# Loading every block of q and k in 2 KB runs and keeping the tokens in (j r) order

## The chip, the core and the metric

The kernel runs on one core of a Trainium2 chip. The core has five engines with their own instruction queues: TensorE (PE in the profile; its weight loads are listed apart as PEld), VectorE (DVE), ScalarE (ACT), GpSimd (POOL) and SyncE (SP), which here only issues DMAs. Engines meet through semaphores alone. The metric is the device time of one execution in microseconds (us), lower is better.

## The reference, cut to what matters

Two layers follow each other. The first is causal attention that keeps, for each query, only the best six chunks of 32 keys; the second is a gated feed-forward layer over the 3072 resulting rows. All inputs and the output are fp32.

```python
# q, k, v: (4, 8, 768, 64): batch, heads, tokens, head_dim
k_min, k_max = min and max of k over each chunk of 32 tokens      # 24 chunks
ub = sum_d maximum(q * k_min, q * k_max)                          # a bound for each query and chunk
ub = where(query's chunk >= chunk, ub, -1e9)
top_chunks = argsort(ub)[..., -6:]
scores = q @ k.T / 8, masked to the selected chunks and to earlier tokens
attn_out = softmax(scores) @ v

x = attn_out as (4 * 768, 512)
xn = x / sqrt(mean(x * x) + 1e-6) * rms_g
out = (silu(xn @ w_gate) * (xn @ w_val)) @ w_out                  # 512 -> 1536 -> 512
```

## The kernel before, in words

The work is cut into 12 blocks: a batch `b` and 256 of its 768 tokens (`m` is 0, 1 or 2), in the order of the list ORDER (L341); `i` is a block's place in that list. For each block and each of two groups `g` of four heads the kernel does the following.

- **Load** (load_qk, L427). A block of q or k is brought to a tile of 128 partitions: four heads of 32 partitions, and for each the two groups, eight values `j`, and 64 numbers. For the first three blocks (PACKED, L351) partition `r` of a head takes the eight consecutive tokens 8r to 8r+7, a run of 2 KB in memory: four DMAs of 128 KB bring one tensor. For the nine other blocks partition `r` takes the tokens 32j + r, eight runs of 256 bytes: eight DMAs of 64 KB. All but those of block 0 are issued by SP. `load_v` brings v.
- **Turn** (L635). DVE transposes 32 by 32 squares, so that the 64 numbers lie on partitions and the tokens along the columns. Column 32j + r then holds token 32j + r in the nine blocks, which is token order, and token 8r + j in the packed ones, which is called (j r) order.
- **Copy to bf16** (half, L640 to L645). ACT or POOL writes `kb` and `qb` in token order; in the packed blocks its read runs over the columns with a step of 32 floats.
- **Choice of chunks.** DVE takes the minimum and maximum of k over each chunk (L650). TensorE multiplies them in fp32 with q and with the positive part of q (relu, L729) (upper_first, L539, for m = 0, upper, L521, for the others), DVE picks the six best and makes a mask from them.
- **Scores** (unit, L763). `kb` is the stationary operand, 128 keys, `qb` the moving one, 128 or 256 queries; four heads run side by side, on 32 partitions each. The mask is added in the same accumulation (L774). ACT takes the exponential (L813), POOL cuts the triangle (L783), TensorE multiplies with v (L839), DVE normalizes.
- **Feed-forward.** The row norm, a transpose of the rows (by TensorE in the first four blocks, by DMA, L899, in the others), the two wide products (L963), tanh on ACT, the products on DVE and POOL (L974 to L984), the output product (L1008) and a store by SP (L1030).

The order is not made by loops at run time. A planner has written down one list of all steps (SEQUENCE, L21), the buffer that each step takes (SLOTS), which engine does a step that several could do (CHOICE), and where matmuls without use stand that keep TensorE busy while it would wait (WARM, keep_busy, L1073 to L1076: place in the list, number, PSUM buffer, 1 for 512 columns and 0 for 128). Plan.run (L201) replays the list. Each engine executes its steps in that order and waits where an operand or a buffer is not ready. The numbers in the calls (0.54, 1.0 and so on) are the planner's costs in us for a step; at run time they have no effect.

Of the kernel before, what the change touches and what calls it, by code (L numbers as in the profile page):

```python
# [12 lines left out]
AXX = mybir.AxisListType.X  # L13
# [8 lines left out]
    29, 3, 4, 5, 44, 45, 0, 14, 21, 32, 6, 7, 34, 37, 35, 36, 64, 15, 17, 31, 55, 57, 65, 12, 16, 23, 13, 26,  # L22
    24, 19, 22, 8, 66, 67, 58, 68, 56, 59, 69, 46, 38, 39, 40, 41, 1, 28, 131, 27, 25, 30, 60, 61, 2, 70, 47,
    62, 71, 63, 72, 105, 106, 107, 147, 73, 96, 138, 140, 150, 148, 52, 53, 48, 49, 50, 51, 42, 43, 97, 139,
    129, 74, 82, 54, 83, 130, 18, 33, 132, 133, 20, 98, 145, 149, 75, 141, 156, 76, 142, 146, 84, 165, 166,
    167, 151, 99, 152, 85, 143, 144, 108, 77, 100, 101, 78, 102, 79, 103, 80, 109, 157, 154, 158, 159, 160,
    161, 162, 111, 110, 81, 104, 86, 87, 88, 112, 90, 113, 116, 135, 89, 93, 91, 92, 117, 94, 95, 118, 168,
    164, 173, 114, 174, 115, 175, 153, 213, 215, 214, 216, 155, 188, 189, 179, 187, 180, 181, 163, 124, 119,
    190, 217, 218, 220, 219, 125, 126, 120, 134, 191, 223, 182, 232, 183, 184, 225, 185, 234, 127, 121, 122,
    123, 128, 169, 196, 1078, 170, 171, 1080, 1084, 197, 198, 235, 186, 1086, 1079, 1082, 226, 172, 202, 192,  # L30
    194, 193, 1081, 230, 1083, 1087, 1072, 1074, 176, 1073, 1085, 227, 137, 228, 203, 204, 1076, 239, 177,
    1075, 236, 237, 261, 178, 195, 241, 229, 238, 242, 1088, 243, 262, 263, 205, 199, 1090, 224, 1089, 200,
    201, 206, 207, 208, 1092, 264, 1093, 265, 209, 1091, 1117, 1096, 1120, 1094, 210, 1102, 136, 231, 1077,
    1095, 1098, 1099, 240, 1104, 211, 1105, 244, 245, 266, 1097, 1100, 296, 301, 302, 288, 290, 298, 293, 289,
    299, 292, 291, 294, 295, 450, 303, 300, 297, 457, 372, 374, 379, 377, 376, 458, 375, 221, 1101, 1103,
    1116, 1106, 1107, 233, 1118, 1119, 1134, 1122, 1136, 1124, 1137, 1125, 246, 247, 315, 306, 308, 317, 1135,
    1129, 1128, 1138, 248, 1130, 1121, 1146, 250, 1148, 1132, 1149, 309, 267, 310, 268, 313, 1123, 251, 1126,
    253, 364, 378, 373, 222, 369, 304, 1147, 1140, 1150, 270, 316, 1142, 271, 273, 324, 1151, 318, 322, 254,
    1127, 311, 319, 1143, 325, 249, 1141, 1108, 1109, 1144, 320, 321, 10, 307, 272, 252, 269, 1145, 387, 312,
    274, 397, 1131, 1110, 1133, 1139, 1112, 255, 256, 275, 276, 257, 277, 1113, 1114, 278, 258, 368, 367, 365,  # L40
    371, 454, 366, 370, 451, 380, 456, 305, 463, 1115, 460, 259, 279, 260, 280, 281, 282, 389, 323, 283, 9,
    326, 327, 328, 1152, 1153, 382, 285, 329, 384, 330, 390, 392, 331, 393, 385, 394, 332, 395, 314, 284, 286,
    383, 287, 1111, 464, 544, 453, 461, 455, 452, 381, 1156, 1157, 1166, 1158, 1168, 1154, 399, 386, 396,
    1169, 334, 335, 337, 1184, 1172, 346, 1186, 1185, 1160, 1174, 347, 345, 349, 1162, 402, 462, 1155, 549,
    403, 545, 459, 400, 465, 401, 536, 539, 548, 333, 391, 336, 398, 338, 348, 350, 1188, 1187, 468, 1189,
    1175, 1161, 342, 1164, 470, 1163, 343, 344, 1165, 1167, 1170, 354, 339, 1190, 355, 476, 340, 356, 341,
    473, 1171, 1178, 1192, 1180, 388, 1193, 1181, 483, 1173, 1176, 1179, 351, 352, 353, 1182, 413, 404, 405,
    406, 1183, 471, 407, 408, 409, 410, 411, 1191, 469, 466, 1159, 542, 467, 538, 537, 475, 1177, 1196, 358,
    357, 359, 361, 360, 485, 1194, 362, 1195, 428, 363, 1200, 1197, 412, 429, 430, 432, 540, 546, 635, 541,
    543, 554, 556, 481, 479, 1204, 1201, 1222, 1202, 1198, 1206, 472, 478, 480, 547, 639, 488, 550, 551, 487,  # L50
    486, 212, 638, 489, 559, 568, 1203, 433, 482, 1207, 414, 1224, 415, 1216, 1205, 1208, 1223, 1226, 417,
    1218, 477, 474, 490, 434, 431, 491, 561, 11, 555, 570, 514, 627, 632, 634, 642, 574, 552, 637, 641, 629,
    573, 562, 1209, 1225, 564, 1219, 1227, 565, 492, 493, 494, 495, 496, 435, 436, 563, 630, 572, 633, 628,
    571, 1199, 416, 569, 418, 566, 484, 1217, 1210, 1220, 499, 419, 1212, 1213, 420, 421, 440, 1211, 1229,
    497, 557, 1214, 1232, 425, 437, 422, 426, 441, 427, 438, 442, 1215, 558, 1228, 423, 424, 439, 498, 444,
    1230, 1234, 567, 1231, 443, 1236, 576, 575, 636, 640, 1237, 650, 660, 505, 1235, 1238, 577, 506, 507, 500,
    445, 1221, 1233, 631, 1239, 578, 446, 579, 645, 1240, 501, 503, 515, 713, 718, 643, 715, 720, 653, 447,
    719, 553, 502, 504, 652, 560, 516, 518, 508, 511, 1241, 448, 647, 1242, 648, 509, 519, 662, 520, 521, 522,
    517, 449, 644, 664, 656, 510, 1244, 526, 1245, 1266, 1246, 580, 512, 581, 513, 527, 528, 582, 584, 1268,
    1255, 523, 1269, 530, 583, 1254, 649, 524, 525, 655, 1256, 529, 665, 666, 657, 812, 654, 646, 651, 531,  # L60
    1272, 1257, 658, 1274, 1275, 659, 593, 1267, 1261, 532, 534, 1258, 594, 595, 1273, 1264, 1276, 1278, 1270,
    721, 724, 726, 722, 717, 723, 663, 667, 668, 728, 727, 819, 1280, 725, 816, 716, 714, 1271, 1281, 533,
    535, 585, 691, 586, 588, 1260, 1279, 669, 590, 1282, 591, 592, 1277, 676, 587, 739, 736, 745, 738, 747,
    740, 1259, 1283, 670, 731, 733, 742, 1292, 1294, 1295, 734, 1305, 589, 1248, 603, 1262, 1308, 604, 606,
    596, 1298, 1300, 1250, 1263, 741, 597, 598, 671, 605, 749, 751, 750, 748, 752, 743, 599, 1293, 1296, 1301,
    1297, 602, 735, 1265, 607, 804, 1243, 810, 813, 814, 906, 1304, 1306, 808, 806, 898, 805, 811, 600, 732,
    746, 661, 744, 1251, 1307, 1309, 608, 609, 610, 1317, 1310, 1299, 1320, 1302, 1312, 672, 601, 807, 809,
    822, 673, 997, 904, 817, 998, 890, 900, 892, 818, 896, 1247, 895, 815, 905, 902, 899, 901, 893, 891, 611,
    612, 613, 674, 1249, 1252, 1253, 1313, 1311, 1314, 1315, 824, 830, 1316, 675, 617, 677, 678, 614, 831,
    679, 753, 1047, 823, 1318, 615, 616, 680, 620, 1284, 618, 619, 835, 833, 1319, 621, 825, 827, 754, 682,  # L70
    755, 837, 622, 1303, 683, 737, 829, 839, 1288, 1285, 684, 1286, 1322, 1324, 894, 989, 897, 991, 903, 623,
    908, 832, 1289, 1323, 697, 913, 826, 1325, 625, 840, 993, 624, 843, 907, 841, 698, 699, 1321, 681, 688,
    689, 756, 757, 910, 690, 909, 834, 626, 1332, 1290, 1326, 692, 693, 695, 915, 1029, 1291, 1287, 842, 1327,
    1328, 758, 759, 760, 836, 1329, 1333, 685, 762, 696, 922, 924, 694, 1330, 1334, 763, 729, 703, 916, 686,
    704, 705, 687, 700, 701, 702, 1336, 1361, 1360, 845, 764, 828, 838, 844, 765, 1338, 1339, 706, 707, 1364,
    1362, 1363, 767, 846, 768, 769, 1366, 1343, 1368, 981, 987, 730, 779, 990, 911, 847, 848, 708, 766, 761,
    780, 781, 783, 1346, 914, 1337, 1342, 1344, 1340, 770, 709, 711, 849, 1369, 1341, 1345, 850, 992, 1331,
    927, 996, 994, 928, 926, 925, 988, 985, 983, 710, 995, 1004, 1335, 930, 1365, 771, 1349, 1352, 772, 1354,
    1348, 1350, 1351, 1367, 1370, 1371, 1006, 917, 1356, 1355, 776, 777, 1357, 1013, 773, 774, 778, 1358, 782,
    1347, 785, 820, 982, 821, 786, 787, 986, 712, 984, 1380, 775, 1359, 1392, 1381, 1384, 784, 1394, 1382,  # L80
    851, 918, 1383, 1395, 919, 852, 788, 789, 1411, 1387, 1390, 1414, 790, 1410, 1353, 912, 1385, 920, 921,
    1015, 853, 929, 923, 1412, 1376, 794, 1413, 1415, 1005, 868, 795, 796, 859, 1377, 1378, 1404, 791, 792,
    793, 798, 860, 861, 797, 1406, 931, 869, 870, 1398, 872, 1400, 932, 933, 799, 1407, 1399, 1393, 854, 1402,
    1014, 1396, 800, 934, 802, 1397, 1401, 935, 855, 857, 936, 1386, 1372, 1405, 1408, 1019, 801, 803, 856,
    956, 999, 1016, 1018, 1017, 937, 858, 944, 1388, 1389, 1409, 865, 862, 866, 867, 863, 864, 945, 946, 1443,
# [1023 lines left out]
```

## Time and profile before

| | us |
|---|---|
| three runs | 305.08, 305.93 (median), 309.50 |
| profiled execution, its device time | 305.02 |
| its span, first to last instruction | 303.3 |
| TensorE busy | 287.6 |
| VectorE busy | 222.4 |
| ScalarE busy | 207.4 |
| GpSimd busy | 150.8 |

The granted TensorE clock was 0.994 of full speed. The core read 28.58 MB from memory and wrote 6.29 MB. The page cuts the span in 40 slices, and shows the DMA engines 70 to 90% and more busy in the first six and under 60% in nearly all that follow. In the profile an instruction is named by its line in the kernel, its engine, its operation and its tiles, output first; "idle before" is the time its engine stood still just ahead of it, and the name behind the arrow is what ended that. The chain is the path of work and waits that ended last, followed back from the last instruction.

### The profile page before, as it was taken

To read this page: it belongs to the slowest core of one execution; us is meant where nothing else is said; L and a number is where in the kernel's file an instruction comes from. 1 tells how busy PE (TensorE), PEld (TensorE's weight loads), DVE (VectorE), ACT (ScalarE), POOL (GpSimd) and SP (SyncE) were. 2 spreads that over 40 slices of the span, in tenths; PEclk is the share of its full clock that TensorE was granted. 3 is DMA by queue.
4 is the path that set the end of the run, shared out by engine and by line. 5 is a ranking of instruction groups with operands and counts; after the bars stand their busy time and mean duration, and the time that the engine had idled before them with its cause. 6 is when DMAs were issued, how large, how long until landed. Compare 5 with 4: busy or idle time off the path is not lost.

```text
span 303.3 us, 11260 instructions
## 1 busy us (share of the span) xinstructions
PE 287.6 (95%) x4629; PEld 212.7 (70%) x4629; DVE 222.4 (73%) x636; ACT 207.4 (68%) x361; POOL 150.8 (50%) x259
## 2 busy tenths in 40 slices
PE   6998959999999999969999999999999999999994
PEld 2455849756867875858875688777787877777763
DVE  2978976989999999886999877768286837353340
ACT  1279974837689985965877896787686696644521
POOL 1878674395664676283445765233664164011610
PEclk9999999999999999997999999999999999999999
DMA  7999997685486448556753858002102003004011
GB/s 196 226 186 261 206 173 147 153 198 145 128 194 158 101 121 151 118 88 152 165 140 84 206 150 164 9 4 63 71 2 71 3 2 106 3 2 139 2 69 70
DMA packets 86387, 35.07 MB, mean 116 GB/s; under 512 B 74816, under 2 KB 81728, under 8 KB 86336
## 3 DMA queue, kind: packets, MB, share of 16 engines
q1 hardware_dynamic: 80736, 29.12, 40.8%
q0 software_dynamic: 4752, 4.72, 9.6%
q10 hardware_dynamic: 848, 0.53, 0.8%
q8 instruction: 36, 0.59, 0.8%
q14 instruction: 15, 0.12, 0.2%
HBM read 28.58 MB, written 6.29 MB: 115 GB/s over the span
## 4 chain that ended last, share of the span: by engine, by line
PE 75%; DVE 11%; issue 3%; SPq 3%; DMA 2%; ACT 2%; POOL 2%; DVEq 0%; POOLq 0%; ACTq 0%
PE F L963 34%; PE F L1008 19%; PE S L763 6%; PE F L839 6%; PE F L1076 4%; PE S L774 2%; SPq L368 2%; PE F L521 2%; DVE tg L974 1%; DVE kx L650 1%; DVE xs L907 1%; DMA xsT<-xs 1%; ACT junk L875 1%; DVE qT L635 1%; DMA kraw<-in_k_dram 1%
## 5 line engine op out<-in xcount | busy, mean ns | idle before, releaser
L813 ACT ACTIVATE pt<-S 128x1024 bf16<-128x1024 f32 (+3 forms) x104 | 85.1, 861 | 23.9 <-PE S L774 20.6
L963 PE MATMUL F<-xsT,wg 128*128 128x256 bf16 (+1 forms) x608 | 73.2, 269 | 4.9 <-DVE kT L635 2.4
L981 POOL TENSOR_TENSOR hh<-tg,vs 128x512 bf16<-128x512 bf16 x43 | 49.7, 1167 | 51.4 <-DVE tg L974 29.1
L963 PE MATMUL F<-xsT,wv 128*128 128x256 bf16 (+1 forms) x608 | 73.1, 269 | 0.1
L974 DVE SCALAR_TENSOR_TENSOR tg<-th,F 128x512 bf16<-128x512 bf16 x72 | 48.4, 681 | 29.3 <-ACT th L970 24.9
L1008 PE MATMUL F<-wo,hh 128*128 128x512 bf16 (+1 forms) x300 | 67.8, 371 | 0.0
L963 PEld LDWEIGHTS <-wg 128*128 128x128 bf16 x608 | 55.8, 98 | 14.4 <-issue 4.1
L963 PEld LDWEIGHTS <-wv 128*128 128x128 bf16 x608 | 55.7, 98 | 9.9 <-issue 0.8
L970 ACT ACTIVATE th<-F 128x512 bf16<-128x512 f32 x72 | 42.2, 599 | 20.2 <-PE F L963 18.9
L1008 PEld LDWEIGHTS <-hh 128*128 128x128 bf16 x300 | 28.0, 98 | 26.3 <-POOL hh L981 0.5
L783 POOL TENSOR_SCALAR_AFFINE_SELECT pt<-pt 128x512 bf16<-128x512 bf16 x48 | 31.4, 659 | 22.9 <-ACT pt L813 22.6
L763 PE MATMUL S<-qb,kb 32*128 32x256 bf16 (+1 forms) x800 | 33.6, 253 | 0.2
L978 ACT ACTIVATE vs<-F 128x512 bf16<-128x512 f32 x43 | 25.2, 601 | 11.6 <-PE F L963 7.1
L650 DVE TENSOR_REDUCE kx<-kT 128x16 f32<-128x512 f32 x48 | 31.6, 671 | 0.2
L839 PE MATMUL F<-VX,pt 128*128 128x65 bf16 x672 | 27.6, 194 | 0.7 <-POOL pt L783 0.7
L839 PEld LDWEIGHTS <-pt 128*128 128x128 bf16 x672 | 25.2, 98 | 3.7 <-POOL pt L783 1.0
L763 PEld LDWEIGHTS <-kb 32*128 32x128 bf16 x800 | 14.2, 92 | 12.3 <-issue 11.1
L983 DVE TENSOR_TENSOR hh<-tg,F 128x512 bf16<-128x512 bf16 x29 | 19.4, 676 | 3.3 <-PE F L963 3.2
L1076 PE MATMUL F<-chunkrow,ident 128*128 128x512 bf16 x73 | 18.7, 408 | 2.9 <-DVE chunkrow L407 2.9
L1023 ACT ACTIVATE osb<-F 128x512 f32<-128x512 f32 (+1 forms) x15 | 8.6, 582 | 18.0 <-PE F L1008 15.5
L774 PE MATMUL S<-mtd,chunkrow 32*128 32x128 bf16 (+2 forms) x384 | 20.8, 203 | 0.0
L774 PE MATMUL S<-mto,chunkrow 32*128 32x128 bf16 (+2 forms) x384 | 20.5, 203 | 0.1
(71 smaller groups left out, 350.8 us busy)
## 6 DMA issues: line engine op xcount, KB each, us to landing
vraw<-in_v_dram SPq DMA_DIRECT2D x24, 256.0 KB, 4.0
out_dram<-osb SPq DMA_DIRECT2D x23, 256.0 KB, 2.4
qraw<-in_q_dram SPq DMA_DIRECT2D x72, 64.0 KB, 2.8
kraw<-in_k_dram SPq DMA_DIRECT2D x72, 64.0 KB, 2.9
QX<-qT SPq DMA_DIRECT2D x32, 64.0 KB, 2.5
wg<-in_moe_w_gate_dram POOLq DMA_DIRECT2D x3, 512.0 KB, 6.9
wv<-in_moe_w_val_dram POOLq DMA_DIRECT2D x3, 512.0 KB, 10.6
wo<-in_moe_w_out_dram POOLq DMA_DIRECT2D x3, 512.0 KB, 7.9
```

Source lines behind the costliest of these rows:

```text
L650: plan.op(f"ext{n}{J}", "DVE", 0.585, 0.67, lambda n=n, op=op: VE.tensor_reduce(out=at(kx)[:, g, n], in_=at(kT).rearrange("p h (j c x) -> ...
L763: TE.matmul(s[a // 2][:, a % 2, c0:c0 + q1 - q0], kbt[r, t, ks], qbt[r, t, q0:q1], start=(t == 0), stop=(t == 1 and not mask), skip_group_ ...
L774: TE.matmul(o, chunkrow[r, BLK * kg + P * e:BLK * kg + P * (e + 1)], mv, start=False, stop=(d == 1), skip_group_check=True)
L783: GE.affine_select(out=d, in_=d, compare_op=ALU.is_ge, fill=0.0, base=0, pattern=[[0, 4], [1, P]], channel_multiplier=-1)
L813: lambda pt=pt, hs=hs, c0=c0, c1=c1, x=sc[hp]: SE.activation(out=at(pt)[:, hs, c0:c1], in_=at(x)[:, :, c0:c1], func=ACT.Exp, scale=SCALE), ...
L839: TE.matmul(o[:, a, :], p_[:, a, off:off + P], vt[:, e, a, :], start=(kb_ == 0 and a == 0), stop=(kb_ == nkb - 1 and a == 3), skip_group_c ...
L963: TE.matmul(at(p_)[:, n * W:(n + 1) * W], w[:, g, ht * P:(ht + 1) * P], at(xT)[:, g, x0:x0 + W], start=(g == 0), stop=(g == NP - 1), skip_ ...
L970: plan.op(f"tanh{U}.{hp}", "ACT", 0.48, 0.6, lambda th=th, gp=gp: SE.activation(out=at(th), in_=at(gp), func=ACT.Tanh, scale=0.5), pri - 0 ...
L974: VE.scalar_tensor_tensor(out=at(tg), in0=at(th), scalar=1.0, in1=at(gp), op0=ALU.add, op1=ALU.mult), pri - 30, reads=[th, gp], writes=[tg ...
L981: "POOL": (1.11, 1.16, lambda tg=tg, vs=vs, hh=hh: GE.tensor_tensor(out=at(hh), in0=at(tg), in1=at(vs), op=ALU.mult)),
L1008: TE.matmul(at(op)[:, cs], at(key)[:, o:o + P], wo[:, ht, cs], start=(ht == 0), stop=(ht == NHT - 1), skip_group_check=True)
L1076: TE.matmul(store["F"][slot][:, 0:x.shape[1]], ident[:], x, start=True, stop=True)
```

## The change

1. All 12 blocks load q and k as the first three did: four DMAs of 128 KB in runs of 2 KB per tensor. PACKED is gone.
2. `qb` is a straight copy and stays in (j r) order. The score matmul reads it through a view that runs over r and then j, so with a step of 32 bf16 numbers (64 bytes). Its output is in token order as before.
3. `kb` is brought to token order in its copy, in all blocks. In the blocks with an odd place (ALONG) the copy runs in the order of its input and writes with a step of 8 bf16 numbers (16 bytes); in the even ones it runs in the order of its output and reads with a step of 32 floats.
4. The bounds' matmuls (upper and upper_first) read fp32 q, and its positive part, with a step of 32 floats or, for the compact positive part of the m = 0 blocks, of 8; the minimum and maximum use the packed form everywhere; relu keeps the (j r) order.
5. SEQUENCE, SLOTS, CHOICE and WARM are new lists. The first fillers are 127 matmuls of 128 columns on `ident` alone instead of 49 of 512 columns on `chunkrow`; of the wide ones behind them there are 41 instead of 24. On each engine the number of instructions changes little otherwise: QX copies POOL 5, ACT 8, DVE 3 (13, 3, 0 before), products hh on POOL 46 (43), on DVE 26 (29).

The core of the diff (the lists are left out):

```diff
 WARM = [
-    (59, 49, 0, 1), (100, 9, 0, 1), (118, 2, 0, 1), (119, 1, 0, 1), (139, 3, 1, 1), (186, 8, 3, 1), (188, 1,
-    2, 1)]
+    (38, 127, 0, 0), (97, 8, 2, 1), (127, 6, 0, 1), (144, 2, 0, 1), (171, 3, 1, 1), (233, 1, 2, 1), (342, 16,
+    0, 1), (343, 5, 2, 1)]
...
+    ALONG = {1, 3, 5, 7, 9, 11}
...
-    PACKED = {0, 1, 2}
...
-            if i in PACKED:
-                sv = src[b].rearrange("(g a) (m r j) d -> a m r g (j d)", a=4, m=NBLK, r=32)[a, m]
-                todo = [(sv, lambda rows=rows: at(key)[rows].rearrange("r g j h d -> r g (j h d)"),
-                         4, 0.104 if i == 0 else 0.12)]
-            else:
-                todo = []
-                for g in range(NG):
-                    sv = src[b, 4 * g + a, BLK * m:BLK * (m + 1), :].rearrange(
-                        "(j r) d -> r j d", r=32)
-                    todo.append((sv, lambda rows=rows, g=g: at(key)[rows, g].rearrange(
-                        "r j h d -> r j (h d)"), 16, 0.019))
...
+            sv = src[b].rearrange("(g a) (m r j) d -> a m r g (j d)", a=4, m=NBLK, r=32)[a, m]
+            dma(f"load {nm}{b}{m}{a}", eng, sv,
+                lambda rows=rows: at(key)[rows].rearrange("r g j h d -> r g (j h d)"),
...
-                qs = [x.rearrange("p h (j c r) -> p h j c r", c=2, r=CH) for x in qs]
+                qs = [x.rearrange("p h (j y c z) -> p h c y z j", y=nj, c=2, z=4) for x in qs]
...
-                                TE.matmul(bank()[e][x:x + 32, k_], BD[b][r, g, n_, p_, :],
-                                          qs[n_][r, p_, :, c, :], start=(n_ == 0), stop=(n_ == 1),
+                                TE.matmul(bank()[e][x:x + 32, k_].rearrange(
+                                              "p (y z j) -> p y z j", y=nj, j=8), BD[b][r, g, n_, p_, :],
+                                          qs[n_][r, p_, c], start=(n_ == 0), stop=(n_ == 1),
...
-            act = lambda: SE.activation(out=natural(at(hb)), in_=order(turned(nm)), func=ACT.Copy)
-            pool = lambda: GE.tensor_copy(natural(at(hb)), order(turned(nm)))
-            flex(f"half {nm}{J}", {"ACT": (1.0, 1.1, act), "POOL": (1.02, 1.06, pool)} if packed else {"ACT": (0.54, 0.63, act), "POOL": (0.57, 0.61, pool)},
+
+            def views():
+                o, x = at(hb), turned(nm)
+                if nm == "k":
+                    o = o.rearrange("p h (r j) -> p h j r", j=8)
+                    x = x.rearrange("p h (j r) -> p h j r", j=8)
+                    if i not in ALONG:
+                        o, x = [y.rearrange("p h j r -> p h r j") for y in (o, x)]
+                return o, x
+
+            act = lambda: (lambda o, x: SE.activation(out=o, in_=x, func=ACT.Copy))(*views())
+            pool = lambda: (lambda o, x: GE.tensor_copy(o, x))(*views())
+            flex(f"half {nm}{J}", {"ACT": (0.54, 0.63, act), "POOL": (0.57, 0.61, pool)},
...
-            kbt, qbt = at(("kb", b, kg, g)), at(qb)
+            kbt, qbt = at(("kb", b, kg, g)), at(qb).rearrange("p t (j r) -> p t r j", j=8)
...
-                ks = slice(P * e, P * (e + 1))
+                ks, qs = slice(P * e, P * (e + 1)), slice(q0 // 8, q1 // 8)
...
-                                  kbt[r, t, ks], qbt[r, t, q0:q1],
+                                  kbt[r, t, ks], qbt[r, t, qs],
```

More of the change, by code (lines that the diff above doesn't have):

```diff
@@ L724, in go @@
                 o, x = qr(), at(qx if m else qT)[:, g]
-                if packed:
-                    o, x = o.rearrange("p h (r j) -> p h r j", j=8), order(x)[:, :, 32 - w // 8:]
-                else:
-                    x = x[:, :, BLK - w:]
+                if not m:
+                    o = o.rearrange("p h (j r) -> p h j r", j=8)
+                    x = x.rearrange("p h (j r) -> p h j r", j=8)[:, :, :, 32 - w // 8:]
                 eng.tensor_scalar(out=o, in0=x, scalar1=HUGE, scalar2=0.0, op0=ALU.min, op1=ALU.max)
@@ L733, in job @@
         yield
-        flex(f"relu{J}", {"POOL": (0.58 if m else 0.36 if packed else 0.25, 0.62 if m else 0.4 if packed else 0.29, relu(GE)),
+        flex(f"relu{J}", {"POOL": (0.58 if m else 0.25, 0.62 if m else 0.29, relu(GE)),
                           "DVE": (0.34 if m else 0.14, 0.42 if m else 0.22, relu(VE))},
```

38 lines of the change are left out of this document (13 added, 25 removed), and 222 rows, old and new, of tables (SEQUENCE, SLOTS).

## The prediction, made before the changed kernel ran

> **What bounds the kernel now.** I read the page first: busy time by engine, then the chain that ended last.
>
> ```profile
> PE 287.6 (95%) x4629; PEld 212.7 (70%) x4629; DVE 222.4 (73%) x636; ACT 207.4 (68%) x361; POOL 150.8 (50%) x259
> ...
> PE 75%; DVE 11%; issue 3%; SPq 3%; DMA 2%; ACT 2%; POOL 2%; DVEq 0%; POOLq 0%; ACTq 0%
> PE F L963 34%; PE F L1008 19%; PE S L763 6%; PE F L839 6%; PE F L1076 4%; PE S L774 2%; SPq L368 2%; PE F L521 2%; DVE tg L974 1%; DVE kx L650 1%; DVE xs L907 1%; DMA xsT<-xs 1%; ACT junk L875 1%; DVE qT L635 1%; DMA kraw<-in_k_dram 1%
> ```
>
> TensorE is busy for 95% of the span and carries 75% of the chain; no other engine is near it. An average hides stages, so I cut the span where the kind of work changes (columns: stretch and its length; busy us and instruction count of PE, PEld, DVE, ACT, POOL; granted clock; DMA share; GB/s).
>
> ```profile
> 0.00:15.40 15.40, 12.54 (x57) 5.32 (x57) 9.14 (x18) 3.59 (x4) 8.41 (x39) 1.00 1.02 211
> 15.40:30.30 14.90, 13.66 (x324) 8.23 (x318) 11.84 (x53) 12.95 (x30) 11.92 (x26) 1.00 1.21 224
> 30.30:65.00 34.70, 31.62 (x480) 25.70 (x478) 29.84 (x67) 23.23 (x46) 20.55 (x35) 1.00 0.89 167
> 65.00:136.00 71.00, 67.90 (x1244) 50.87 (x1240) 66.82 (x207) 57.43 (x103) 43.31 (x70) 1.00 0.62 140
> 136.00:190.00 54.00, 52.99 (x957) 40.46 (x958) 44.86 (x143) 41.30 (x68) 29.34 (x45) 0.97 0.64 150
> 190.00:264.00 74.00, 74.00 (x1325) 56.90 (x1326) 46.22 (x128) 55.32 (x87) 29.59 (x40) 1.00 0.12 34
> ```
>
> The DMA engines are full only up to about 65 us. Between 65 and 136 us PE is idle for 71.00 - 67.90 = 3.1 us, between 136 and 190 us for 1.0 us, between 190 and 264 us for nothing. So a faster load has at most a few us to win, while every us that a TensorE instruction gets longer after 65 us lands on the end almost whole.
>
> **The loads.** Blocks 0 to 2 load packed already; the other nine change from eight 64 KB loads of 256-byte runs each for q and for k to four of 128 KB.
>
> ```profile
> qraw<-in_q_dram SPq DMA_DIRECT2D x72, 64.0 KB, 2.8
> kraw<-in_k_dram SPq DMA_DIRECT2D x72, 64.0 KB, 2.9
> ...
> kraw<-in_k_dram SPq DMA_DIRECT2D x10, 128.0 KB, 4.6
> ```
>
> 144 issues become 72 (9 blocks x 2 tensors x 4). One issue occupies SP's queue like this, and the longest idle time of PE behind a load is this:
>
> ```profile
> 123.58 0.44 SPq L368
> ...
> 136.12 1.22 PE L963 MATMUL F<-xsT,wg 128*128 128x256 bf16 x5 [2.37 <-DVE kT L635]
> ```
>
> 72 x 0.44 = 32 us leave SP's queue, ahead of the stores, the QX copies and the transposing loads that share it. But that queue shows on the chain with 2%, and what it can win is the idle time of PE: 3.1 us before 65 us, 3.1 and 1.0 us behind. I take 2 us of these 7.2, because the 2.37 us row is a k load's wait and the others have other releasers; the bounds are 0 and 7. Once k comes earlier, DVE (94% busy from 65 to 136 us, 66.82 of 71.00) is what is late next.
>
> **The head.** Before, 49 wide fillers keep PE busy ahead of its first score matmul; they end later than the data, of which the last is the bf16 copy of q on ACT, ended at 11.65 + 1.05 = 12.7 us.
>
> ```profile
> 11.65 2.10 ACT L642 ACTIVATE qb<-qT 128x512 bf16<-128x512 f32 x2 [7.46 <-DVE qT L635]
> 2.86 12.50 PE L1076 MATMUL F<-chunkrow,ident 128*128 128x512 bf16 x49 [2.86 <-DVE chunkrow L407]
> 15.29 0.29 PE L763 MATMUL S<-qb,kb 32*128 32x128 bf16 x8
> L1076 PEld LDWEIGHTS <-ident 128*128 128x128 bf16 x73 | 7.2, 103 | 11.6 <-issue 3.7 <-POOL eps L392 1.5
> ```
>
> After, 127 fillers of 128 columns, which need the identity alone. Each still loads its weights, at 103 ns at most 127 x 0.103 = 13.1 us from about 1.5 us, so they end by 14.6 us; at half that pace they end at 8 us and data are the bound, at about 12.7 us. So the first scores come 0.7 to 2.6 us earlier; I take 1.5 us. The fillers behind the head grow from 24 to 41 wide ones, 17 x 12.50/49 = 4.3 us; they stand where PE would wait, so I count nothing, and +4 us as the bound if the waits are gone.
>
> **The copies to bf16.** Before, the packed blocks turn (j r) into token order in the copy of q and of k; the others copy straight. Both prices stand in the trace (columns: count, min/median/max ns, first and last start):
>
> ```profile
> L642 ACT ACTIVATE qb<-qT x4: 1078/1092/1112, 11.6 to 24.2; 128x512 bf16<-128x512 f32 x4
> L642 ACT ACTIVATE qb<-qT x9: 614/622/651, 67.2 to 207.0; 128x512 bf16<-128x512 f32 x9
> L643 POOL CAST kb<-kT x3: 1062/1069/1073, 8.0 to 13.9; 128x512 bf16<-128x512 f32 x3
> L643 POOL CAST kb<-kT x10: 604/611/617, 73.9 to 232.2; 128x512 bf16<-128x512 f32 x10
> ```
>
> The reordering copy reads with a step of 32 floats and costs 1.09 instead of 0.62 us on ACT, 1.07 instead of 0.61 on POOL: 0.47 us more. Removed: 12 of them (blocks 0 to 2, two head groups, q and k), 5.6 us. Added: the k copies, read with that step in the six even blocks (12 x 0.47 = 5.6 us), and in the six odd ones written with a step of 16 bytes, which no row shows: 0 to 0.47 us each, so up to 5.6 us. Spread over ACT (68%) and POOL (50%) behind a saturated PE this is hidden; what it can cost is a late k, and the planner's list still counts 0.54 us for each. I take +0.5 us, bounds 0 and +5. The min and max reductions (L650) read runs of four floats in the packed blocks and took the same 0.67 us there. No price changes for the relu.
>
> **TensorE's reads of q.** Now the large term. q in bf16 stays in (j r) order and the score matmul (L763) reads it as its moving operand with a step of 32 elements, 64 bytes, 256 or 128 columns at a time; all 800 score matmuls change.
>
> ```profile
> L763 PE MATMUL S<-qb,kb 32*128 32x256 bf16 x544 | 25.8, 271 | 0.0
> L763 PE MATMUL S<-qb,kb 32*128 32x128 bf16 x256 | 9.2, 215 | 0.2
> ...
> 65.00:136.00 71.00, 8.90 (x208) 3.83 (x208) 1.00 0.62 140
> 136.00:190.00 54.00, 8.19 (x192) 3.33 (x192) 0.97 0.64 150
> 190.00:264.00 74.00, 11.81 (x272) 4.88 (x272) 1.00 0.12 34
> ...
> 101.91 0.40 PE L763 MATMUL S<-qb,kb 32*128 32x256 bf16 x8
> 102.14 0.22 PE L774 MATMUL S<-mtd,chunkrow 32*128 32x128 bf16 x4
> ```
>
> Four run side by side on four groups of rows: eight wide ones hold PE for 102.14 - 101.91 = 0.23 us, 0.115 us per four, 0.45 ns per column. So L763 streams 136 x 256 + 64 x 128 = 43,000 columns, 19.3 us. 672 of the 800 lie behind 65 us, where PE has no slack. No row shows a bf16 operand read with a step. The nearest rows differ:
>
> ```profile
> 15.51 0.44 PE L539 MATMUL F<-qT,BO 64*64 64x32 f32 x16
> 15.76 0.47 PE L539 MATMUL F<-qraw,BO 64*64 64x32 f32 x14
> 16.02 0.23 PE L539 MATMUL F<-qT,BO 64*64 64x32 f32 x2
> ...
> L813 ACT ACTIVATE pt<-S 128x1024 bf16<-128x1024 f32 x48 | 47.3, 1025 | 11.2 <-PE S L774 11.0
> L813 ACT ACTIVATE pt<-S 128x256 bf16<-128x256 f32 x8 | 2.8, 381 | 2.8 <-PE S L763 2.8
> ...
> 0.00:303.30 303.30, 9.35 (x512) 7.19 (x512) 0.99 0.52 116
> ```
>
> L539 reads fp32 q with a step of 128 bytes (qT) and straight (qraw) at one pace: 16 in 0.25 us, then 14 in 0.26 us. That says a step is free, at a slow pace: a row group takes 8 x 32 = 256 elements in 0.25 us, 0.98 ns each, twice a score column's 0.45. At 0.98 ns the 43,000 columns need 42 us, +23 us. ACT's own slope is (1025 - 381)/768 = 0.84 ns per element, and the stepped copy adds 0.47 us/512 = 0.92 ns, so 1.76 ns, 2.1 times the straight one; the same 1.76 ns per column on PE gives 76 us, +56 us. Bounds: 0 and +56 us; nothing speaks for a gain. I take the ratio of the copies, about two, and +20 us: it lies under the +23 us that PE's own rows allow. L521 (last row, 9.35 us) reads fp32 q with a step of 128 bytes too; its nearest row, L539, shows no price, so 0, with +9 us if it doubled.
>
> The Trainium skill, "SBUF — State Buffer", section Specifications (TRN2), says that memory lines are 16 bytes and that full bandwidth needs at least two accesses to a line. By it a 64-byte step slows the moving read, without a figure; the copies on ACT and POOL agree (1.09 against 0.62 us), while the fp32 rows of L539, slower per column to begin with, cannot tell. By the rule the sum is the forecast's or that of ACT's price below; by L539's rows taken alone it is the 302 us of the first rival.
>
> **The sum**, against the profiled execution's own 305.0 us (span 303.3; the median of the runs, 305.9, is 0.3% above): 305.0 - 2.0 (loads) - 1.5 (head) + 0.5 (copies) + 20 (score matmuls) = 322 us.
>
> **The rivals.**
> - A stepped read is free at bf16 as L539 has it at fp32. Then 305.0 - 2.0 - 1.5 + 0.5 = 302 us, not slower. It decides if four wide score matmuls still take 0.115 us. For it: L539's equal paces. Against it: both copies that double. Bounds 296 (all 7.2 us of idle time and 2.6 of the head) to 310 (fillers and late copies).
> - PE pays the 1.76 ns of ACT per column: 302 + 56 = 358 us, and with L521 doubled 367. For it: one memory serves all engines, and POOL pays the same extra as ACT. Against: 0.98 ns with a step is on record for PE.
> - The read is free, but the order was written with 0.54 us per k copy, 24 of them take up to 1.09, and PE waits for k about block by block: 302 + 9 (24 x 0.47 = 11 us less what idle time absorbs) = 311 us. Against: DVE and PE stand between.
> - The loads do not get faster: a 128 KB load took 4.6 us, two 64 KB ones overlap at 2.9. Then the 2 us for loads are missing, inside each range above.
>
> **How the numbers follow.** Forecast 322 us: 0.42, its own range 312 to 335 (+12 to +30 for the score reads and L521). Free read 302: 0.33. ACT's price 358: 0.17. Late copies 311: 0.08. The range 298 to 340 holds the first, nearly all of the second and the fourth, and leaves ACT's price out: 0.42 + 0.31 + 0.08 = 0.81. Two per cent of 305.9 is 6 us, about what a measurement can tell from no change: faster than 299.8 is a quarter of the free case, 0.08; up to 312 its rest and half of the fourth, 0.29; slower 0.63.
>
> **What would show it.** In the profile after: the distance from the first of eight wide score matmuls to the first mask matmul behind them: 0.45 us here, 0.23 if free, 0.9 at ACT's price. L763 with a chain share near 12%. k copies at 1.09 us in even blocks. First scores near 13.8 us. SP's queue with 72 fewer load issues and PE's 2.37 us idle behind the k load gone. Wrong would make it: reads that cost nothing, or scores that grow while PE's gaps shrink by as much.

## The result

The changed kernel takes 362.7 us (median; 360.3 to 363.8) against 305.5 us: a ratio of 1.190, 95% interval 1.178 to 1.202. It is slower, as forecast, but by 57 us and not by 17. The page of the changed kernel, busy time and chain (most of its lines behind the lists are 17 less than before; L746 is the score matmul, L507 the bounds' matmul, L1059 the fillers):

```profile
PE 348.5 (97%) x4724; PEld 228.4 (63%) x4724; DVE 223.6 (62%) x641; ACT 215.1 (60%) x362; POOL 163.6 (45%) x253
...
PE 89%; DMA 3%; DVE 3%; ACT 2%; POOL 1%; issue 1%; ACTq 0%; DVEq 0%
PE F L946 35%; PE S L746 21%; PE F L991 18%; PE F L822 6%; PE F L507 4%; PE S L757 3%; PE F L1059 2%; DMA kraw<-in_k_dram 2%; DMA qraw<-in_q_dram 1%; DVE xs L890 1%; ACT kb L627 1%; DVE tg L957 1%; DVE kT L610 1%; PE F L902 0%; PE F L522 0%
```

TensorE's busy time grew from 287.6 to 348.5 us, 61 us, nearly the whole difference of the spans (360.3 - 303.3 = 57.0 us); TensorE's weight loads (PEld) took 15.7 us more, and no other engine moved by more than 13 us. The score matmul's share of the chain went from 6 to 21%. By form, in the groups of the changed kernel:

```profile
L746 PE MATMUL S<-qb,kb 32*128 32x256 bf16 x544 | 68.7, 594 | 0.0
...
L746 PE MATMUL S<-qb,kb 32*128 32x128 bf16 x256 | 19.4, 380 | 2.6 <-ACT kb L627 1.4 <-ACT qb L627 1.1
```

The distance named in the prediction, from the first of eight wide score matmuls to the first mask matmul, and of eight narrow ones, in the timeline of the changed kernel (start, length, instruction, count):

```profile
103.38 1.03 PE L746 MATMUL S<-qb,kb 32*128 32x256 bf16 x8
104.23 0.24 PE L757 MATMUL S<-mtd,chunkrow 32*128 32x128 bf16 x4
104.30 0.23 PE L757 MATMUL S<-mto,chunkrow 32*128 32x128 bf16 x4
104.36 0.60 PE L746 MATMUL S<-qb,kb 32*128 32x128 bf16 x8
104.77 0.22 PE L757 MATMUL S<-mtd,chunkrow 32*128 32x64 bf16 x4
```

0.85 us instead of 0.23, 1.66 ns per column instead of 0.45; the narrow ones take 0.41 us. In sum 68 x 0.85 + 32 x 0.41 = 71 us against 19.3: +52 us. The bounds' matmul grew too; 64 of them, in the timeline and with the next instruction behind:

```profile
128.28 0.66 PE L507 MATMUL F<-QX,BD 64*32 64x128 f32 x16
128.72 0.68 PE L507 MATMUL F<-qraw,BD 64*32 64x128 f32 x16
129.16 0.70 PE L507 MATMUL F<-QX,BD 64*32 64x128 f32 x16
129.62 0.70 PE L507 MATMUL F<-qraw,BD 64*32 64x128 f32 x16
130.25 1.02 PE L746 MATMUL S<-qb,kb 32*128 32x256 bf16 x8
```

1.97 us for 64. Before, it was this:

```profile
131.80 0.45 PE L521 MATMUL F<-QX,BD 64*32 64x128 f32 x16
...
132.91 0.40 PE L763 MATMUL S<-qb,kb 32*128 32x256 bf16 x8
```

1.11 us. Eight blocks do that once each: +6.9 us. Other signs: the first scores start at 11.27 us (15.29 before), and the copies of k are slow in a way that no row of before showed. ACT's and POOL's copies in the changed kernel (count, min/median/max ns, first and last start):

```profile
L627 ACT ACTIVATE kb<-kT x8: 1101/1892/2532, 12.4 to 238.1; 128x512 bf16<-128x512 f32 x8
L628 POOL CAST kb<-kT x16: 1060/1806/2505, 7.9 to 269.4; 128x512 bf16<-128x512 f32 x16
L628 POOL CAST qb<-qT x14: 608/613/868, 16.1 to 259.7; 128x512 bf16<-128x512 f32 x14
```

About 1.1 us where the copy reads with a step (even blocks), 2.5 us where it writes with one (odd blocks), 0.61 us for the straight copy of q.

The transfers did what was meant of them: 52,979 packets instead of 86,387, and PE was busy for 79.95 of the 80 us from 80 to 160 us. An earlier k had nothing left to win there, since PE itself had become that much longer.

### The profile page after: what moved, and what is told of

Read it like the earlier page. It is cut to its first block, busy times and chain, and to the rows that moved or that the text cites. A ratio compares the mean times of both kernels' runs of the same rounds, so it can differ in the third digit from the quotient of the medians.

```text
span 360.3 us, 11359 instructions
## 1 busy us (share of the span) xinstructions
PE 348.5 (97%) x4724; PEld 228.4 (63%) x4724; DVE 223.6 (62%) x641; ACT 215.1 (60%) x362; POOL 163.6 (45%) x253
## 2 busy tenths in 40 slices
DMA packets 52979, 35.08 MB, mean 97 GB/s; under 512 B 36800, under 2 KB 43712, under 8 KB 52928
## 4 chain that ended last, share of the span: by engine, by line
PE 89%; DMA 3%; DVE 3%; ACT 2%; POOL 1%; issue 1%; ACTq 0%; DVEq 0%
PE F L946 35%; PE S L746 21%; PE F L991 18%; PE F L822 6%; PE F L507 4%; PE S L757 3%; PE F L1059 2%; DMA kraw<-in_k_dram 2%; DMA qraw<-in_q_dram 1%; DVE xs L890 1%; ACT kb L627 1%; DVE tg L957 1%; DVE kT L610 1%; PE F L902 0%; PE F L522 0%
## 5 line engine op out<-in xcount | busy, mean ns | idle before, releaser
L964 POOL TENSOR_TENSOR hh<-tg,vs 128x512 bf16<-128x512 bf16 x46 | 53.2, 1161 | 86.2 <-ACT vs L961 56.7
L746 PE MATMUL S<-qb,kb 32*128 32x256 bf16 (+1 forms) x800 | 86.6, 526 | 2.6 <-ACT kb L627 1.4
L946 PE MATMUL F<-xsT,wg 128*128 128x256 bf16 (+1 forms) x608 | 71.9, 270 | 0.0
L946 PEld LDWEIGHTS <-wv 128*128 128x128 bf16 x608 | 54.9, 98 | 9.1 <-issue 0.4
L757 PEld LDWEIGHTS <-chunkrow 32*128 32x128 bf16 x768 | 23.9, 110 | 46.4 <-issue 41.1
L961 ACT ACTIVATE vs<-F 128x512 bf16<-128x512 f32 x46 | 27.0, 598 | 26.3 <-PE F L946 22.3
L628 POOL CAST kb<-kT 128x512 bf16<-128x512 f32 x16 | 28.6, 1788 | 5.5 <-DVE kT L610 5.5
L966 DVE TENSOR_TENSOR hh<-tg,F 128x512 bf16<-128x512 bf16 x26 | 17.7, 685 | 15.2 <-PE F L946 9.4
L746 PEld LDWEIGHTS <-kb 32*128 32x128 bf16 x800 | 14.3, 92 | 15.7 <-issue 12.0
L757 PE MATMUL S<-mtd,chunkrow 32*128 32x128 bf16 (+2 forms) x384 | 23.1, 220 | 0.0
L837 DVE RECIPROCAL rden<-F 128x4 f32<-128x4 f32 x48 | 8.1, 175 | 21.4 <-PE F L822 17.2
```

The lines of the kernel that those rows point to most:

```text
L628: pool = lambda: (lambda o, x: GE.tensor_copy(o, x))(*views())
L746: TE.matmul(s[a // 2][:, a % 2, c0:c0 + q1 - q0], kbt[r, t, ks], qbt[r, t, qs], start=(t == 0), stop=(t == 1 and not mask), skip_group_che ...
L757: TE.matmul(o, chunkrow[r, BLK * kg + P * e:BLK * kg + P * (e + 1)], mv, start=False, stop=(d == 1), skip_group_check=True)
L946: TE.matmul(at(p_)[:, n * W:(n + 1) * W], w[:, g, ht * P:(ht + 1) * P], at(xT)[:, g, x0:x0 + W], start=(g == 0), stop=(g == NP - 1), skip_ ...
L964: "POOL": (1.11, 1.16, lambda tg=tg, vs=vs, hh=hh: GE.tensor_tensor(out=at(hh), in0=at(tg), in1=at(vs), op=ALU.mult)),
```

## The experiments

The theory at this point: the 64-byte step of the score matmul's moving read costs PE 1.66 ns per column, and this is the loss. The rival: the new recorded order, with k copies that take up to 2.5 us where it counts on 0.54, makes everything late.

### e1: q in token order by its copy, all else as changed

```diff
-                if nm == "k":
+                if True:
                     o = o.rearrange("p h (r j) -> p h j r", j=8)
                     x = x.rearrange("p h (j r) -> p h j r", j=8)
-                    if i not in ALONG:
+                    if nm == "q" or i not in ALONG:
...
-            kbt, qbt = at(("kb", b, kg, g)), at(qb).rearrange("p t (j r) -> p t r j", j=8)
+            kbt, qbt = at(("kb", b, kg, g)), at(qb).rearrange("p t (r j) -> p t r j", j=8)
```

> One part undone: the copy of q to bf16 puts it in token order (its read steps by 32 floats, as the packed blocks did before), so the score matmul reads straight columns; everything else is the changed kernel's, its order too. Theory 1 (the step in the score matmul's read is the loss): eight wide score matmuls take 0.23 us again instead of 0.85, L746 loses 52 us, and the time falls from 362.7 to about 311 us; what is left above 305.5 is L507 (8 x 0.8 = 6 us). Rival (the new order and the late k copies are the loss): PE waits instead, the time stays above 340 us.

Measured: 315.0 us, ratio 1.030 (1.019 to 1.040). 47.7 us are gone. Groups of this run:

```profile
L746 PE MATMUL S<-qb,kb 32*128 32x256 bf16 x544 | 25.7, 271 | 0.0
L627 ACT ACTIVATE qb<-qT 128x512 bf16<-128x512 f32 x10 | 11.1, 1112 | 6.6 <-DVE qT L610 6.5
L746 PE MATMUL S<-qb,kb 32*128 32x128 bf16 x256 | 9.2, 215 | 3.7 <-ACT qb L627 1.6 <-ACT kb L627 1.3 <-ACT pt L796 0.6
```

The score matmuls are back at their old busy times, to 0.1 us, while the copies of q now cost 1.11 us and the order is still the new one. PE's busy time fell by 348.5 - 295.9 = 52.6 us; the span by 46.9, because PE's idle time rose from 11.8 to 17.5 us. The time is 4 us above the 311 that the theory gave and far below the rival's 340: the theory holds.

### e2: the changed code in the order of before

```diff
-SEQUENCE, SLOTS, CHOICE, WARM = ...  # the lists of the changed kernel
+SEQUENCE, SLOTS, CHOICE, WARM = ...  # those of the kernel before; a joined load stands at its first half's place
```

> The changed code with the recorded order, buffers, engine choices and fillers of the kernel before (of the two loads that became one, the first one's place is kept). Theory 1: the order matters little, 355 to 368 us. Rival (the new order costs most of it): under 335 us.

Measured: 357.9 us, one run, span 355.7. The order is not the loss: the old one takes the span down by 4.6 us of 57. The k copies of 2.5 us are still in this run; it is e1, which keeps them and the new order and is yet 47.7 us shorter, that clears them.

### e3: the order of before, q and k in token order by stepped reads

```diff
-    ALONG = {1, 3, 5, 7, 9, 11}
+    ALONG = set()
```

(on e2, with the edit of e1)

> As the run before this one, but q in token order by its copy and every k copy in the order of its output (ALONG empty): what remains of the change is the 2 KB loads of all blocks, the reordering copies of all q and k, and the stepped fp32 reads of the bounds' matmuls. Theory 1: 305.5 - 2 (loads) + 6 (L507) = about 309 us, 305 to 314. If the loads were worth more than the 2 us given to them: under 305 us.

Measured: 310.2 us, ratio 1.013 (1.005 to 1.020), as expected of the theory. The time is above before, since the bounds' matmul still reads fp32 with a step. Its busy time in this run, in one stretch over everything (length; busy us and count of PE and PEld; granted clock; DMA share; GB/s), is to be held against the 9.35 us of before:

```profile
0.00:400.00 400.00, 16.69 (x512) 10.46 (x512) 0.99 0.38 88
```

### e4: what a step costs on TensorE

A part of the first fillers of the kernel before gives way to series of 12 matmuls, each on a line of its own. Work is added; the series are read by themselves. (The comments in this cut and in those of e8 and e9 give lines and meaning; they are not in the kernels.)

```diff
+        lambda: TE.matmul(*stepped(1), start=True, stop=True),         # L1097, straight, 512 columns
+        lambda: TE.matmul(*half_row(2), start=True, stop=True),        # L1098 to L1102: 256 columns,
+        lambda: TE.matmul(*half_row(4), start=True, stop=True),        #   every 2nd, 4th, 8th, 16th, 32nd element
+        lambda: TE.matmul(*half_row(8), start=True, stop=True),
+        lambda: TE.matmul(*half_row(16), start=True, stop=True),
+        lambda: TE.matmul(*half_row(32), start=True, stop=True),
+        lambda: TE.matmul(*stepped(32, 2), start=True, stop=True),     # L1103 to L1105: runs of 2, 4, 8 in every 32
+        lambda: TE.matmul(*stepped(32, 4), start=True, stop=True),
+        lambda: TE.matmul(*stepped(32, 8), start=True, stop=True),
+        lambda: TE.matmul(*spread_out(2), start=True, stop=True),      # L1106, L1107: output with a step of 2, 8 fp32
+        lambda: TE.matmul(*spread_out(8), start=True, stop=True),
+        lambda: TE.matmul(*wide_type(1), start=True, stop=True),       # L1108 to L1110: fp32, step 1, 4, 32
+        lambda: TE.matmul(*wide_type(4), start=True, stop=True),
+        lambda: TE.matmul(*wide_type(32), start=True, stop=True),
```

> The kernel before, with part of its first fillers replaced by series of 12 matmuls each, which read the same constant tile in different ways: bf16, 256 columns, with steps of 2, 4, 8, 16 and 32 elements (4 to 64 bytes); runs of 2, 4 and 8 elements every 64 bytes; straight reads with the output written with a step of 2 and of 8 fp32; fp32, straight and with steps of 4 and 32. Work is added, so its total time says nothing. Theory A (a read pays per 16-byte line): up to a step of 4 elements near 0.45 ns per column, 8 and more 1.7 ns, runs of 2 half of that per column, runs of 4 near free. Theory B (any step costs, for two neighbours are read together): a step of 2 costs as much as one of 32. Outputs with a step: free if PSUM takes a column at a time, over twice as long if its lines count. fp32: straight 1.0 ns per column and pass, step 32 1.7.

The series in the timeline of this run:

```profile
10.91 2.75 PE L1097 MATMUL F<-chunkrow,ident 128*128 128x512 bf16 x12
13.50 1.52 PE L1098 MATMUL F<-chunkrow,ident 128*128 128x256 bf16 x12
14.86 2.88 PE L1099 MATMUL F<-chunkrow,ident 128*128 128x256 bf16 x12
17.56 5.59 PE L1100 MATMUL F<-chunkrow,ident 128*128 128x256 bf16 x12
22.98 5.71 PE L1101 MATMUL F<-chunkrow,ident 128*128 128x256 bf16 x12
28.50 5.35 PE L1102 MATMUL F<-chunkrow,ident 128*128 128x256 bf16 x12
33.68 5.03 PE L1103 MATMUL F<-chunkrow,ident 128*128 128x480 bf16 x12
38.53 2.61 PE L1104 MATMUL F<-chunkrow,ident 128*128 128x480 bf16 x12
40.98 2.11 PE L1105 MATMUL F<-chunkrow,ident 128*128 128x384 bf16 x12
42.93 5.31 PE L1106 MATMUL F<-chunkrow,ident 128*128 128x512 bf16 x12
48.03 5.36 PE L1107 MATMUL F<-chunkrow,ident 128*128 128x512 bf16 x12
53.32 5.39 PE L1108 MATMUL F<-chunkrow,ident 128*64 128x256 f32 x24
58.55 11.04 PE L1109 MATMUL F<-chunkrow,ident 128*64 128x256 f32 x24
69.41 10.50 PE L1110 MATMUL F<-chunkrow,ident 128*64 128x256 f32 x24
```

From start to next start, divided by the columns (the instruction behind the last series starts at 79.84 us). Each of the 12 fp32 matmuls leaves two records, called passes here:

| read or written | ns per column |
|---|---|
| bf16 straight | 0.42 |
| bf16, step 2 elements (4 bytes) | 0.44 |
| step 4 (8 bytes) | 0.88 |
| step 8, 16, 32 (16, 32, 64 bytes) | 1.76, 1.80, 1.69 |
| runs of 2, 4, 8 in every 64 bytes | 0.84, 0.43, 0.42 |
| bf16 straight, output with a step of 2, 8 fp32 | 0.83, 0.86 |
| fp32 straight, per pass | 0.85 |
| fp32, step 4, 32 (16, 128 bytes), per pass | 1.77, 1.70 |

Theory A holds, with one correction: the price is 1.7 ns for every 16 bytes that the read touches, and it is hidden as long as the elements taken from them need as long themselves. That is four bf16 columns (4 x 0.42 = 1.7); the step of 4, which takes two elements from 16 bytes, costs twice, where the expectation had it free. Theory B, two neighbours read together, falls: a step of 2 is free. The Trainium skill's figure of at least two accesses to a line for full bandwidth ("SBUF — State Buffer", section Specifications (TRN2)) is too low for bf16 on TensorE: two to a line (the step of 4) take 0.88 ns per column, and it takes four to be free.

A slower clock is not the reason. The granted clock was 0.50 in the series with steps of 16 and 32, 0.76 in the one with runs of 2, 0.94 at the step of 8 and 1.00 in all others. But the step of 32 has the same price at a granted clock of 1.00 in e9 (0.43 us for 256 columns, 1.68 ns each), and so nearly has the score matmul of the changed kernel (1.66). So the price of a stepped read did not change with the granted clock between 0.50 and 1.00.

### e5: fp32 q read straight, sums written with a step

fp32 takes 0.85 ns per pass anyway, and a stepped output 0.86. So the step of the bounds' matmul can move from its read to its output. On e3:

```diff
-                qs = [x.rearrange("p h (j y c z) -> p h c y z j", y=nj, c=2, z=4) for x in qs]
+                qs = [x.rearrange("p h (j y c z) -> p h c j y z", y=nj, c=2, z=4) for x in qs]
...
-                                              "p (y z j) -> p y z j", y=nj, j=8), BD[b][r, g, n_, p_, :],
+                                              "p (y z j) -> p j y z", y=nj, j=8), BD[b][r, g, n_, p_, :],
```

> The order of before, 2 KB loads, q and k in token order by their copies, and the bounds' matmul (L507) reading fp32 q straight, in runs of four, and writing its sums with a step of 8 fp32 instead. Theory (fp32 takes 0.85 ns per column and pass anyway, a stepped output 0.86): 64 matmuls of L507 take 1.1 us again instead of 1.8, eight blocks give back 6 us, 304 us, ratio 0.98 to 1.00 to before. Rival (the two prices add): 64 take 2 us or more and the time stays at 310 or above, ratio 1.01 or more.

Measured: 304.3 us, ratio 0.987 (0.982 to 0.993): a little under the kernel before, clear of the noise but by less than 2%. The bounds' matmul is at its old busy time (over everything, as above):

```profile
0.00:400.00 400.00, 9.74 (x512) 7.33 (x512) 0.99 0.37 88
```

The stage from 65 to 136 us, the one in which PE waited 3.1 us before, in this run (columns as in the prediction):

```profile
65.00:136.00 71.00, 69.65 (x1194) 51.39 (x1200) 65.76 (x209) 58.25 (x101) 47.36 (x71) 1.00 0.53 140
```

PE idles for 1.35 us there, the DMA engines are busy for 0.53 of it instead of 0.62 at the same 140 GB/s, and SP's queue no longer appears on the chain:

```profile
PE 71%; DVE 12%; ACT 7%; POOL 4%; issue 3%; DMA 1%; DVEq 0%; ACTq 0%; POOLq 0%
```

The profiled executions don't show the whole 1.3%. This one took 305.9 us against 305.0 before; PE's idle time in all fell from 15.7 to 13.8 us, and its busy time rose from 287.6 to 289.9.

### e6 and e7: the new order, mended step by step

e6 is e1 with `ALONG = set()`; e7 is e6 with the edit of e5.

> As e1 (the changed kernel with q in token order by its copy), but the k copies of the odd blocks read with a step too instead of writing with one: 12 copies fall from 2.5 to 1.08 us, 17 us of ACT and POOL. Theory (they are hidden behind PE): 0 to 3 us less than e1's 315, so 312 to 315. Rival (late k copies hold PE up in the new order): 300 to 307.

> e6 with the bounds' matmul as in e5, so the new order with everything mended. If the new order is as good as the old one: 304 to 307 and within 1% of e5. If the new order is worse by itself: 2% or more above e5.

Measured: e6 313.4 us, ratio 1.021 (1.016 to 1.025); e7 306.9 us, ratio 1.001 (0.997 to 1.005). So the 2.5 us copies cost little in spite of some 15 us more of ACT and POOL (387.7 us of busy time in e1, 373.2 in e6): 1.6 us by the medians, 0.9% or 2.7 us by the ratios to before, which are the better measure as e1 and e6 did not run side by side. The intervals overlap, so it may be nothing. The new order, everything else equal, is worse than the old one: by 2.5 us by the medians (306.9 against 304.3) and by 1.4%, about 4 us, by the ratios, whose intervals do not meet. That lies between the two cases named ahead of the run: the order has a price, and it is small beside the 57 us.

### e8: what a step costs in a write

Copies of 256 bf16 elements from one tile, four times over, on ACT (L1082 to L1088), DVE (to L1095) and POOL (to L1102), at the start of the kernel before, with the written step in each line:

```diff
+        SE.activation(out=cells(narrow[0], 1), in_=x, func=ACT.Copy)   # L1082: bf16, step 1; then 2, 4, 8
+        SE.activation(out=cells(broad[0], 1), in_=x, func=ACT.Copy)    # L1086: fp32, step 1; then 2, 4
```

> The kernel before with added copies of 256 elements at its start, four times over, on ACT, DVE and POOL: bf16 read straight, written as bf16 with steps of 1, 2, 4 and 8 elements (2, 4, 8, 16 bytes), and as fp32 with steps of 1, 2 and 4 (4, 8, 16 bytes). Work is added, so its total time says nothing. Theory (a write pays per line as a read does, 1.7 ns): step 8 adds about 0.9 ns per element, 0.24 us, on ACT and POOL. Rival (a bf16 write with a step costs more, as the 2.5 us of the k copies in the odd blocks say): 4 to 5 ns per element at a step of 8, 1 us or more, and fp32 with the same 16 bytes will tell whether the element's size or the step counts.

ACT's rows (count, min/median/max ns):

```profile
L1082 ACT ACTIVATE pt<-chunkrow x4: 410/412/414, 13.5 to 26.3; 128x256 bf16<-128x256 bf16 x4
L1083 ACT ACTIVATE pt<-chunkrow x4: 490/492/493, 13.9 to 26.8; 128x256 bf16<-128x256 bf16 x4
L1084 ACT ACTIVATE pt<-chunkrow x4: 768/770/777, 14.4 to 27.3; 128x256 bf16<-128x256 bf16 x4
L1085 ACT ACTIVATE pt<-chunkrow x4: 1342/1344/1351, 15.2 to 28.1; 128x256 bf16<-128x256 bf16 x4
L1088 ACT ACTIVATE QX<-chunkrow x4: 659/662/666, 17.3 to 30.2; 128x256 f32<-128x256 bf16 x4
```

The rival holds: a bf16 write with a step of 16 bytes takes 0.93 us more than a straight one for 256 elements, 3.6 ns each, and 0.66 us in all as fp32 with the same 16 bytes. So the element's size counts and not the step alone. POOL has 1.32 us for the same bf16 row; DVE's rows scatter too much to be read (0.19 to 1.63 us for the straight one). The three engines ran at once, and an fp32 write right behind a stepped one was slower than the next (0.71 against 0.43 us on ACT), so these are prices with neighbours. Why a small element is dearer to write is open.

### e9: one stream or the partition

Series as in e4, with half of the output rows (64) each; a pair is two matmuls on different output columns that read the same cells:

```diff
+        lambda: TE.matmul(*narrow(1, 0), start=True, stop=True),       # L1111: one, straight, 256 columns
+        lambda: TE.matmul(*narrow(32, 0), start=True, stop=True),      # L1112: one, step of 32 elements
+        lambda: pair(1),                                               # L1107 and L1108: two, straight
+        lambda: pair(32),                                              # L1107 and L1108: two, step of 32
+        lambda: TE.matmul(*wide_type(2), start=True, stop=True),       # L1115: fp32, step 2
+        lambda: TE.matmul(*wide_out(8), start=True, stop=True),        # L1116: fp32, output with a step of 8
+        lambda: TE.matmul(*wide_type(1), start=True, stop=True),       # L1117: fp32, straight
```

> Which price the fp32 rows of L539 could have shown. The kernel before, with series of 12 (pairs: 24) added at its start: bf16 matmuls onto 64 output rows, 256 columns, straight and with a step of 32 elements, one alone or two side by side on the two halves of the output rows; fp32 with a step of 2, fp32 straight with its output written with a step of 8, fp32 straight. Work is added, so its total time says nothing. Theory (the line price holds for each stream of a matmul, and two streams share nothing): a stepped pair takes 0.43 us for its two times 256 columns, as one alone does, so 0.85 ns per element that a partition gives out, which is what L539's 0.98 ns was. Rival (the price holds for the partition): a stepped pair takes 0.86 us. fp32 with a step of 2 and with a stepped output: 0.22 us for 256 columns and pass, as straight.

The single stepped matmuls are on L1112 (count, min/median/max ns, first and last start):

```profile
L1112 PE MATMUL F<-chunkrow,ident x12: 590/607/608, 11.6 to 16.4; 128*64 128x256 bf16 x12
```

Twelve starts, one every (16.4 - 11.6)/11 = 0.44 us (0.43 with the starts to a hundredth, 11.63 and 16.35). The straight singles (L1111) and the fp32 series, in the timeline:

```profile
10.30 1.50 PE L1111 MATMUL F<-chunkrow,ident 128*64 128x256 bf16 x12
...
23.46 5.61 PE L1115 MATMUL F<-chunkrow,ident 128*64 128x256 f32 x24
28.91 5.34 PE L1116 MATMUL F<-chunkrow,ident 128*64 128x256 f32 x24
34.09 5.34 PE L1117 MATMUL F<-chunkrow,ident 128*64 128x256 f32 x24
```

The straight singles start every (11.63 - 10.30)/12 = 0.11 us. Out of the stepped pairs, one half of the output rows on L1107, the other on L1108, these are the ends of a stretch of ten pairs:

```profile
18.52 0.61 PE L1107 MATMUL F<-chunkrow,ident 128*64 128x256 bf16 x1
18.66 0.61 PE L1108 MATMUL F<-chunkrow,ident 128*64 128x256 bf16 x1
...
23.03 0.61 PE L1107 MATMUL F<-chunkrow,ident 128*64 128x256 bf16 x1
```

A stepped pair starts every (23.03 - 18.52)/10 = 0.45 us, where a single one took 0.43 to 0.44. So the price is that of one stream, and two streams that read the same partitions run side by side at almost no loss. fp32 with a step of 2 takes 0.23 us per pass of 256 columns, with a stepped output 0.22, straight 0.22: both free, as expected.

### e10: the stepped copies alone

```diff
-            act = lambda: SE.activation(out=natural(at(hb)), in_=order(turned(nm)), func=ACT.Copy)
-            pool = lambda: GE.tensor_copy(natural(at(hb)), order(turned(nm)))
+            by = lambda x: x.rearrange("p h (r j) -> p h r j", r=32)
+            along = lambda x: x.rearrange("p h (j r) -> p h r j", r=32)
+            act = lambda: SE.activation(out=by(at(hb)), in_=along(turned(nm)), func=ACT.Copy)
+            pool = lambda: GE.tensor_copy(by(at(hb)), along(turned(nm)))
```

> The kernel before, with the copies of q and k to bf16 reading with a step of 32 floats in all blocks instead of three (the nine other blocks then get their tokens in a wrong order; the work is the same otherwise): 36 copies cost 0.47 us more on ACT and POOL, 17 us in all. Theory (hidden behind PE): 0 to 2 us more than before, ratio 1.000 to 1.007, and then the gain of e5 is the loads' alone. Rival (late k copies hold PE up): 4 us or more, and the loads are worth that much more than e5 shows.

Measured: ratio 1.0005 (0.994 to 1.007). The added work on ACT and POOL (372.5 us of busy time in all, 358.2 before) hides behind PE, with an uncertainty of 2 us. So e5's 1.3%, about 4 us, is what the loads are worth by the ratios, with some 2 us of uncertainty each from e5 and from e10.

Where they win it is not shown. This run loads as before, and yet in its profiled execution (311.8 us) PE idles for only 1.60 us between 65 and 136 us, and its chain has SP's queue at 0%, as in e5:

```profile
65.00:136.00 71.00, 69.40 (x1166) 51.17 (x1170) 65.89 (x208) 57.88 (x101) 47.25 (x71) 1.00 0.59 143
```

So neither of these two signs can be put down to the loads.

## Why the prediction was wrong, step by step

- **The bound.** Right: PE sets the end, and behind 65 us its instructions' time lands on it: +61 us of PE busy time, +57 us of span.
- **TensorE's reads of q.** Here it failed. The step was "I take the ratio of the copies, about two, and +20 us: it lies under the +23 us that PE's own rows allow". The term measured +52 us. Both halves of the sentence were wrong. What two engines have in common was not the ratio but the time: ACT's stepped copy pays 1.76 ns per element, the score matmul 1.66, and PE, twice as fast to begin with, loses four times instead of two. And the 0.98 ns of L539, taken as a limit, were the elements of two matmuls that read the same partitions at once; e9 shows a pair of stepped streams at 0.45 us per 256 columns, 0.9 ns per element for the partition and 1.7 to 1.8 for a stream. Per stream L539 gave 2 x 0.98 = 1.96 ns, above the price, so it could not show it and gave no limit below it. (e9's pairs are bf16 and L539 is fp32; why its matmuls of 32 columns take 1.96 ns straight as well was not measured.) The rival with ACT's price per element had the size right, with 358 to 367 us; it had a chance of 0.17 and lay outside the range. That ACT and PE pay nearly the same time for a stepped element comes out of their rows (ACT's as an estimate from two of them); that one cause stands behind both is not shown.
- **L521.** Costed at 0, bound +9; it measured +6.9 us, and 2.6% of the time lies between e3 and e5 (ratios 1.013 and 0.987), which differ in nothing else. The nearest row, L539, misled for the same reason.
- **The loads.** -2 us, bounds 0 and 7; about -4 us by the ratios of e5 and e10, 1.9 us less of PE's idle time in e5's profiled execution. The sign was right and the size lies within the bounds. The way that was given for it, less waiting of PE and a shorter queue of SP, stays open: e10 shows both signs without the new loads.
- **The head.** -1.5 us, at most 2.6; the first scores came 4.0 us earlier (11.27 us). The fillers took 0.077 us each ((11.27 - 1.47)/127), and the straight copy of q, begun sooner and 0.46 us shorter, ended at 11.0 us instead of 12.7. Taking the 12.7 us as fixed was the mistake. PE waits 1.1 us for the next copy of q right behind, so part of it is given back. The fillers in all, which the sum put at nothing, are 2.4 us more of PE's busy time (18.7 us before, 9.9 and 11.2 after).
- **The copies.** +0.5 us, hidden: right by e10 for the stepped reads; what the stepped writes cost (1.6 or 2.7 us by e6) is not clear of the noise. The bound of 0.47 us for the stepped write was wrong: it takes 1.9 us more.
- **The new order.** Not in the sum beyond its head; +2.5 us by the medians and about 4 by the ratios (e7 against e5), 4.6 us in e2's one run. Late k copies, the third rival, were not the loss either: e1 keeps them and the order, and 47.7 of the 57 us are gone.
- **Chances.** Slower had 0.63 and came, but only 0.17 of it stood on the price that acted. With the sizes measured since, the sum gives 305.0 - 4 (loads) + 52 (scores) + 7 (bounds) + 1.6 (odd blocks' copies) + 2.5 (order) = 364 us, or 367 with the ratios' 2.7 and 4; the profiled execution took 362.1. The terms come from separate runs, so this shows that they suffice, not that each is exact.

## What to carry to other kernels

Price a stepped operand in time per 16 bytes touched, not as a ratio: find the time that one stepped element takes (here an estimated 1.76 ns on ACT, 1.7 on TensorE) and hold it against what the reading engine needs for the elements it takes there. On TensorE, at 0.42 ns per bf16 column, the step slows a read four times, on ACT, at 0.84 ns, about twice. So a layout change is best paid for where time is hidden (a copy on ACT or POOL, e10), and a step can be moved to the side of a matmul that has room (the output of an fp32 matmul, e5). And a pace read off rows that overlap is a sum over streams: divide by their number before it is used as a limit.

## What the runs showed that was not expected

- Four bf16 columns per 16 bytes make a stepped or broken moving read free: a step of 2 elements or runs of 4 (0.44 and 0.43 ns per column), while a step of 4, or runs of 2, doubles it (0.88, 0.84).
- Two matmuls on different output columns read the same partitions with a step at full price each, side by side (0.45 us per pair against 0.43 to 0.44 alone).
- The price of a stepped read did not follow the granted clock: 1.69 ns per column at 0.50 (e4, step of 32) and 1.68 at 1.00 (e9).
- A bf16 write with a step of 16 bytes costs ACT and POOL 2.5 us for 512 elements against 0.6 straight, more than twice a stepped read of fp32 (1.1 us).
- Writing a bf16 matmul's sums with a step of 2 or 8 fp32 doubles its time (0.83 and 0.86 ns per column); for fp32 operands it is free (0.22 us for 256 columns and pass).
